# A query tile's fetch later in SyncE's queue, and one output projection a pair group later, in a fused attention and feed-forward block

## The chip, the core and the metric

The kernel runs on one core of one Trainium2 chip. The metric is the device time of one execution in microseconds (us); a lower one is better. The engines are named as in the profile: PE (TensorE) multiplies matrices into PSUM, DVE (VectorE), ACT (ScalarE) and POOL (GpSimd) do elementwise work, and SP (SyncE) issues most of the transfers (DMA), in the order in which they stand in its queue. Matrices in SBUF and PSUM lie on 128 partitions. PSUM has 8 banks; `pair(i)` in the code is banks 2i and 2i+1.

## The reference

One transformer block over S = 2048 rows of D = 576 values, all in bf16. Cut to what matters:

```python
mod = silu(c) @ w_mod            # six rows of 576: sa, ca, ga, sb, cb, gb
h = layernorm(x) * (1 + ca) + sa
q, k, v = split(h @ wqkv)        # 32 heads of 18
phi(u) = concat(softmax(u @ w_phi), softmax(-(u @ w_phi)))   # 36 features per head
kv = phi(k)^T v ;  z = sum(phi(k))
o = (phi(q) @ kv) / (phi(q) @ z + 1e-6)
x = x + ga * (o @ wo)
h = layernorm(x) * (1 + cb) + sb
x = x + gb * (relu(h @ w1) @ w2)        # 576 -> 4608 -> 576
```

The attention is linear: all keys and values are first summed into one small matrix `kv` per head, and then each row of queries needs only that matrix. So a tile of rows can go through its attention and its feed-forward part without the other tiles, once `kv` is complete.

## The kernel before, in words

The 2048 rows are 16 tiles of 128, taken two by two in 8 blocks (b = 0 to 7). The program has two parts.

The first part is a list of small jobs in a hand-written order (`ORDER`, L44). It loads everything, makes the features of the keys and of all queries, sums `kv`, and takes tiles 0 and 1 through attention, output projection and second layer norm. The features of the queries (`eq(u)` for query tile u) do not all fit in SBUF. From tile 4 on they go out to DRAM (`q_out`, L334) and come back by `q_in(u)` (L337, in the profile `RT<-eqd`, L338) into one of three buffers, number u % 3. So query tiles 4 and 7 share a buffer. `q_fin(u)` (L351) does what turns a fetched tile into an operand: `q_sm` sums the features on DVE (L283, L342), `q_pool` multiplies on POOL (L345, L290), and `q_turn` has a DMA transpose issued by SP (L349, `RE<-RT`; 9 chunks of 128 columns).

The second part is a loop over the blocks. `l1` (L694) is the first feed-forward layer: nine groups u = 0 to 8, each of 36 matmuls (L682) into one PSUM pair, followed by `relu`, which reads that pair with ACT (L690, L691) and DVE (L692). `l2` (L720) is the second layer, written as seven half-size products (L729) with sums of weight parts as operands; DVE makes those sums (`t_part`, L465, and L707, L737). The attention of a later block's two tiles is threaded into this by hooks: a hook is called ahead of each group of `l1` and at each ninth matmul of `l2`, and what it emits stands at that place in every engine's order.

For a tile t the steps are: `attend(t)`, that is `num_mm` on PE (L390) and `num_o` on DVE (L397, L398), which leave the attention's result in o_sb; `o_turn(t)`, a small copy on ACT (L794) and a DMA transpose issued by SP (L402, `oT<-o_sb`; 5 chunks); `project`, the output projection on PE (`wo_full`, L800, 16 matmuls for two tiles, and `wo_rest`, L807, 4 matmuls); `add_res`, the residual sum on DVE (L412); `bn` (L239, L240) and `norm2`, the second layer norm, which ends with another DMA transpose (L402, `h<-xn`).

In block 0 the hook is `b0_l1` (L833). Before group u = 0 and u = 1 it calls `q_next(4)` and `q_next(5)` (L780). `q_next` first issues the fetch that the call before left in `held`, then does `q_fin`, then notes the next fetch. So `q_next(4)` does `q_fin(4)` and notes 7; `q_next(5)` does `q_in(7)`, then `q_fin(5)`, and notes 8. SP's order there is: transpose of query tile 4 (`q_turn(4)`), `q_in(7)`, `q_turn(5)`, and then at u = 3 `o_turn(2)` and `o_turn(3)`. `q_in(7)` writes the buffer that `q_turn(4)` reads. At u = 6 the hook projects tiles 2 and 3 into pairs 2 and 0, ahead of the group's matmuls, and at u = 7 it adds the residuals. The nine groups of block 0 use the pairs 2, 0, 2, 0, 1, 3, 1, 3, 2 (L890). In the later blocks the hooks `in_l1` and `in_l2` do the same steps at other places, with `project` between the blocks (L893).

No scheduler moves anything: each engine takes its instructions in the order in which the program text emits them, and waits on semaphores where data is not yet there.

Of the kernel before, what the change touches and what calls it, by code (L numbers as in the profile page):

```python
# [62 lines left out]
def tile_block(ctx, tc, a, out):  # L63
# [22 lines left out]
    NEQ, NE, NV, NL = 6, 5, 4, 3  # L86
# [70 lines left out]
    def pair(i):  # L157
        return PS[:, 2 * i:2 * i + 2, :]
# [77 lines left out]
    def bn(n, t):  # L236
        s = st[:, t % 4]
        for hf in range(2):
            dve.bn_stats(out=s[:, hf, :], in_=x_sb[:, t, hf * HD:(hf + 1) * HD])  # L239
        dve.bn_aggr(out=mv[:, n, t, :], in_=s)  # L240
# [96 lines left out]
    def q_in(u):  # L337
        sp.dma_start(EL[:, u % NL, :], eqd[:, u, :])  # L338

    def q_sm(u):  # L340
        sums(eq(u), Rq[:, u % 2, :])
        dve.reciprocal(out=rq[:, u % 2, :], in_=hs(Rq[:, u % 2, :], 1))  # L342

    def q_pool(u):
        pool.tensor_tensor(out=ratq[:, u % 2, :], in0=hs(Rq[:, u % 2, :], 0), in1=rq[:, u % 2, :], op=ALU.mult)  # L345
        minus(pool, eq(u), ratq[:, u % 2, :])

    def q_turn(u):
        sp.dma_start_transpose(ET[:, u % NET], eq(u).rearrange("p (c f) -> p c f", f=P))  # L349

    def q_fin(u):  # L351
        q_sm(u)
        q_pool(u)
        q_turn(u)
# [55 lines left out]
    def add_res(t, pr):  # L410
        x = v2(x_sb[:, t, :])
        dve.tensor_tensor(out=x, in0=x, in1=pr[:, :, 0:HD], op=ALU.add)  # L412
# [48 lines left out]
    def t_part(i, k):  # L461

        j = slice(6 * k, 6 * k + 6)
        eng, o, p, q = ((dve, T1, B12, B11), (dve, T2, B22, T1), (dve, T4, B21, T2), (dve, T3, B12, B22))[i]
        eng.tensor_tensor(out=o[:, j, :], in0=p[:, j, :], in1=q[:, j, :], op=ALU.subtract)  # L465
# [312 lines left out]
    held = []  # L778

    def q_next(q):  # L780

        if held and held[0] < NT:
            q_in(held[0])
        del held[:]
        if q < NT:
            q_fin(q)
            held.append(q + NL)

    def attend(t, pr):
        num_mm(t, pr)  # L790
        num_o(t, pr)

    def o_turn(t):
        act.activation(out=o_sb[:, t % 2, D:640], in_=o_sb[:, t % 2, 512:D], func=ACT.Copy)  # L794
        turn_dma(oT[:, t % 2], o_sb[:, t % 2, :])
# [14 lines left out]
    def project(t, prs):  # L810
        for i in range(2):
            wo_full(t + i, prs[i])
        for i in range(2):
            wo_rest(t + i, prs[i])
# [5 lines left out]
    def norm2(t):  # L820
        ln2_rs(t)
        ln2_apply(t)
        i = t % 2
        turn_dma(h2[:, t // 2 % 2, :, i * P:(i + 1) * P], xn[:, i, :])
# [7 lines left out]

    def b0_l1(u):  # L833
        if u < 2:
            q_next(4 + u)
        if u == 2:
            attend(2, pair(1))
            attend(3, pair(3))
        if u == 3:
            o_turn(2)  # L840
            o_turn(3)
        if u in (0, 3, 4):
            t_part(1, (0, 3, 4).index(u))
        if u in (5, 6):
            t_part(3, u - 5)
        if u == 6:
            project(2, (pair(2), pair(0)))
        if u == 7:
            add_res(2, pair(2))
            add_res(3, pair(0))  # L850
            bn(1, 2)
        if u == 8:
            bn(1, 3)
            norm2(2)
# [34 lines left out]
    for b in range(NB):  # L889
        l1(b, (2, 0, 2, 0, 1, 3, 1, 3, 2) if b == 0 else (2, 1, 0, 3, 2, 1, 0, 3, 2), in_l1(b) if b else b0_l1)  # L890
        l2(b, in_l2(b))
        if b + 2 < NB:
            project(2 * b + 4, WO)  # L893
# [103 lines left out]
```

## Time and profile before

| | us |
|---|---|
| median of 3 timed runs | 391.26 |
| lowest and highest | 390.72, 391.53 |
| the profiled execution | 390.21 |
| its span, first to last instruction | 388.4 |
| PE busy in it | 379.6 |
| DVE busy in it | 238.1 |

The profile is of one execution. Times in its rows are us from the start of the span; a row of the timeline gives start, duration, engine, line, operation, the tiles written and read, and how often. A bracket at its end gives how long the engine had been idle and who released it. Block 0's first layer lies at about 92 to 118 us, its second layer at about 118 to 134; the later blocks follow one after another, some 36 us each. In rows of windows the columns are the stretch, its length, the busy time of PE, PEld (the loading of weights), DVE, ACT and POOL with the number of instructions, then the granted clock of PE as a share of full speed, the mean busy share of the 16 DMA engines and the GB/s that they moved.

### The profile page before, as it was taken

The page shows a single profiled execution, that of the slowest core. Times are in us where ns is not written, and L with a number is a line of the kernel's source. Part 1 is how long each engine was busy: PE and PEld are TensorE (multiplying, and loading weights), DVE is VectorE, ACT ScalarE, POOL GpSimd, SP SyncE. Part 2 cuts the span into 40 slices and gives each one's busy share as a digit, 9 for nine tenths or more (in the row PEclk, how much of TensorE's full clock was granted, in tenths as well). Part 3 has the DMA queues.
Part 4 walks back from the last instruction along what each step waited for, and adds up shares of the span by engine and source line. Part 5 has one row for each costly group of instructions (what it writes and reads, how often), then busy time and mean ns, then how long its engine had stood idle before and what let it go on. Part 6 is the DMA issues. An engine that isn't in the chain of part 4 may idle for free.

```text
span 388.4 us, 11401 instructions
## 1 busy us (share of the span) xinstructions
PE 379.6 (98%) x4901; PEld 313.3 (81%) x4901; DVE 238.1 (61%) x439; ACT 186.5 (48%) x449; POOL 123.7 (32%) x195
## 2 busy tenths in 40 slices
PE   8999999999799999999999999999999999999996
PEld 4877788888668788788888887887788888878875
DVE  2899998788929568527743872596177526422243
ACT  2789997689413544505631571256045505622410
POOL 2078889831101402230232124123303230042023
PEclk9999999999989999999999999999999999999999
DMA  7995799798903108401710342064207103001000
GB/s 301 420 417 200 264 385 358 138 251 272 154 19 71 42 17 128 91 32 37 152 34 32 93 95 34 32 108 95 35 19 115 44 30 47 19 0 35 2 2 30
DMA packets 56276, 45.16 MB, mean 116 GB/s; under 512 B 46625, under 2 KB 49314, under 8 KB 55458
## 3 DMA queue, kind: packets, MB, share of 16 engines
q1 hardware_dynamic: 55938, 44.25, 42.2%
q8 instruction: 38, 0.62, 0.7%
q10 hardware_dynamic: 288, 0.19, 0.2%
q14 instruction: 12, 0.10, 0.1%
HBM read 27.38 MB, written 5.90 MB: 86 GB/s over the span
## 4 chain that ended last, share of the span: by engine, by line
PE 86%; DMA 5%; ACT 3%; DVE 3%; issue 1%; POOL 1%; SPq 0%; POOLq 0%; DVEq 0%
PE PS L682 36%; PE PS L729 31%; PE PS L273 10%; PE PS L800 4%; DMA x_sb<-in_xk_dram 2%; ACT RT L278 2%; PE PS L390 2%; DMA R<-in_wkT_dram 2%; DMA oT<-o_sb 1%; PE PS L323 1%; DVE Rk L283 1%; PE PS L807 1%; PE PS L407 1%; DVE st L239 1%; ACT RT L511 0%
## 5 line engine op out<-in xcount | busy, mean ns | idle before, releaser
L682 PE MATMUL PS<-h,R 64*128 64x256 bf16 (+1 forms) x2628 | 143.7, 268 | 0.0
L682 PEld LDWEIGHTS <-R 64*128 64x128 bf16 x2628 | 126.6, 94 | 16.0 <-issue 0.5
L729 PEld LDWEIGHTS <-RH 128*128 128x128 f16 x846 | 81.7, 98 | 21.9 <-issue 1.7
L690 ACT ACTIVATE RH<-PS 128x256 f16<-128x256 f32 x72 | 27.8, 386 | 130.4 <-PE PS L682 130.3
L729 PE MATMUL PS<-R,RH 128*128 128x288 bf16 (+1 forms) x558 | 73.2, 286 | 0.0
L717 POOL TENSOR_TENSOR yt<-yt,gb_row 128x288 f32<-128x288 f32 x23 | 24.9, 1082 | 142.5 <-DVE yt L716 142.5
L692 DVE SCALAR_TENSOR_TENSOR RH<-PS,RH 128x256 f16<-128x256 f32 x72 | 29.6, 415 | 47.4 <-ACT RH L690 47.4
L278 ACT ACTIVATE RT<-PS,rs 128x576 bf16<-128x576 f32 x64 | 42.9, 747 | 2.2 <-PE PS L273 1.8
L691 ACT ACTIVATE RH<-PS 128x512 f16<-128x512 f32 x72 | 42.7, 594 | 0.0
L716 DVE TENSOR_TENSOR yt<-PS,RS 128x288 f32<-128x288 f32 x23 | 10.5, 456 | 46.5 <-PE PS L729 46.5
L729 PE MATMUL PS<-RT,RH 128*128 128x288 f16 x288 | 37.9, 286 | 0.0
L829 ACT ACTIVATE h<-h,mod 128x256 bf16<-128x256 bf16 x63 | 32.8, 590 | 0.0
L273 PE MATMUL PS<-RH,R 116*128 116x288 bf16 x240 | 32.5, 286 | 0.2 <-DVE RH L519 0.2
L345 POOL TENSOR_TENSOR ratq<-Rq,rq 128x32 f32<-128x32 f32 x16 | 4.8, 298 | 87.3 <-DVE rq L342 87.3
L273 PE MATMUL PS<-RH,RT 116*128 116x288 bf16 x240 | 31.9, 286 | 0.2 <-ACT RT L278 0.2
L239 DVE BATCH_NORM_STATS2 st<-x_sb 128x6 f32<-128x288 bf16 x64 | 25.8, 444 | 3.4 <-DMA x_sb<-in_xk_dram 3.4
L273 PEld LDWEIGHTS <-R 116*128 116x128 bf16 x240 | 22.7, 98 | 6.2 <-issue 0.6
L273 PEld LDWEIGHTS <-RT 116*128 116x128 bf16 x240 | 22.9, 98 | 5.8 <-issue 0.3
L733 ACT ACTIVATE RS<-PS 128x288 f32<-128x288 f32 x24 | 9.9, 411 | 32.6 <-PE PS L729 32.6
L718 POOL TENSOR_TENSOR x_sb<-yt,x_sb 128x288 bf16<-128x288 f32 x31 | 22.7, 731 | 5.8 <-DVE yt L714 4.0
L283 DVE TENSOR_REDUCE Rq<-RT 128x64 f32<-128x1152 bf16 x16 | 21.5, 1344 | 0.9 <-DMA RT<-eqd 0.9
L283 DVE TENSOR_REDUCE Rk<-RT 128x64 f32<-128x1152 bf16 x16 | 21.3, 1336 | 0.9 <-ACT RT L278 0.7
(117 smaller groups left out, 414.1 us busy)
## 6 DMA issues: line engine op xcount, KB each, us to landing
R<-in_w_dram SPq DMA_DIRECT2D x4, 1152.0 KB, 8.4
eqd<-RT SPq DMA_DIRECT2D x12, 288.0 KB, 2.1
RT<-eqd SPq DMA_DIRECT2D x12, 288.0 KB, 3.1
R<-in_w2b_dram SPq DMA_DIRECT2D x2, 1296.0 KB, 8.1
R<-in_w2a_dram SPq DMA_DIRECT2D x3, 864.0 KB
out_dram<-x_sb SPq DMA_DIRECT2D x15, 144.0 KB, 1.7
RT<-in_xT_dram SPq DMA_DIRECT2D x2, 640.0 KB
x_sb<-in_xk_dram SPq DMA_DIRECT2D x3, 288.0 KB, 7.7
```

Of the source, the lines that this page charges most:

```text
L239: dve.bn_stats(out=s[:, hf, :], in_=x_sb[:, t, hf * HD:(hf + 1) * HD])
L273: pe.matmul(pr[:, k, 0:HD], lhsT=xt(t, ck), rhs=w[0:R, ck, k * HD:(k + 1) * HD], start=(ck == 0), stop=(ck == NC - 1))
L278: act.activation(out=E.rearrange("p (b h s e) -> p b h s e", b=2, s=2, e=DH)[:, :, :, s, :], in_=pr[:, :, 0:HD].rearrange("p b (h e) -> p ...
L283: dve.tensor_reduce(out=Rr, in_=E.rearrange("p (c e) -> p c e", e=DH), axis=AXX, op=ALU.add)
L682: pe.matmul(PS[:, 2 * u + hf, n * 256 + o:n * 256 + o + w], lhsT=w1[b0:b0 + 64, c, j * P:(j + 1) * P], rhs=hb[b0:b0 + 64, c, o:o + w], sta ...
L690: act.activation(out=A11[:, j, :], in_=lo[:, :, 0, :], func=ACT.Relu)
L691: act.activation(out=A2[:, j, :, :], in_=PS[:, 2 * u + 1, :].rearrange("p (n s f) -> p n s f", n=2, s=2), func=ACT.Relu)
L692: dve.scalar_tensor_tensor(out=U3[:, j, :], in0=lo[:, :, 1, :], scalar=0.0, in1=A11[:, j, :], op0=ALU.max, op1=ALU.subtract)
L717: pool.tensor_tensor(out=y, in0=y, in1=gb_row[:, c], op=ALU.mult)
L718: pool.tensor_tensor(out=x_sb[:, t, c], in0=y, in1=x_sb[:, t, c], op=ALU.add)
L729: pe.matmul(PS[:, bank, 0:HD], lhsT=am[:, j, :], rhs=bm[:, j, :], start=first and j == 0, stop=(j % 9 == 8), skip_group_check=True)
L829: act.activation(out=o, in_=o, func=ACT.Identity, scale=mod(1, c), bias=mod(0, c))
```

## The change

```diff
     def b0_l1(u):
         if u < 2:
-            q_next(4 + u)
+            q_fin(4 + u)
+        if u == 5:
+            q_in(7)
+            held.append(5 + NL)
         if u == 2:
             attend(2, pair(1))
             attend(3, pair(3))
...
         if u in (5, 6):
             t_part(3, u - 5)
-        if u == 6:
+        if u == 7:
             project(2, (pair(2), pair(0)))
-        if u == 7:
             add_res(2, pair(2))
             add_res(3, pair(0))
             bn(1, 2)
```

At u = 0 and u = 1 the hook now does only `q_fin(4)` and `q_fin(5)`. The fetch `q_in(7)` comes at u = 5, and `held` holds 8 from there on as before, so the later blocks see no difference. SP's order becomes `q_turn(4)`, `q_turn(5)`, `o_turn(2)`, `o_turn(3)`, `q_in(7)`. On PE the 20 matmuls of the projection of tiles 2 and 3 move from before the 36 matmuls of group u = 6 to behind them. The order of instructions on DVE, ACT and POOL is the same as before, and no instruction is added or left out. Some semaphores that name a transfer change their number, since they are dealt out in SP's order.

## The prediction

> **What bounds the kernel now.** I read the page first, for the busy shares and the 40 slices.
>
> ```profile
> PE 379.6 (98%) x4901; PEld 313.3 (81%) x4901; DVE 238.1 (61%) x439; ACT 186.5 (48%) x449; POOL 123.7 (32%) x195
> ...
> PE   8999999999799999999999999999999999999996
> ...
> PEclk9999999999989999999999999999999999999999
> ```
>
> TensorE (PE) is busy 98% of the span, and only slice 11 of its row (97.1 to 106.8 us) shows a real hole; the granted clock, PEclk, is below 9 in one slice alone, the next. Time can be gained only in that hole, or by shortening PE's own work. The view of PE's waits over the whole span names the hole: one wait of 2.9 us, for the DMA transpose that fills oT. The next waits are 1.3 us (the kernel's start) and 0.3.
>
> ```profile
> PE PS L800 <- DMA oT<-o_sb: 2.9, 1, 2.9
> PE PS L234 <- POOL eps_t L226: 1.3, 1, 1.3
> PE PS L258 <- ACT RT L278: 0.3, 1, 0.3
> ```
>
> PE's timeline there (start, duration) shows that the first-layer groups u=2 to 5 end at 96.74 + 8.03 = 104.77. Then PE waits until 107.71, when `project(2)` begins.
>
> ```profile
> 96.74 8.03 PE L682 MATMUL PS<-h,R 64*128 64x256 bf16 x144
> 107.71 3.03 PE L800 MATMUL PS<-wo_sb,oT 128*128 128x288 bf16 x16 [2.94 <-DMA oT<-o_sb]
> ```
>
> The chain that ended last gives the stretch without overlaps. The first four rows are this block, the last three the same pieces one block on: 16 + 4 projection matmuls and 9 groups (324 matmuls).
>
> ```profile
> 107.71 3.03 PE PS L800 x16
> 110.74 0.59 PE PS L807 x4
> 111.33 6.38 PE PS L682 x108
> 117.72 2.31 PE PS L729 x18
> ...
> 134.01 1.96 PE PS L800 x16
> 135.97 0.35 PE PS L807 x4
> 136.32 17.68 PE PS L682 x324
> ```
>
> So the same work is slower after the hole. The projection takes 3.03 + 0.59 = 3.62 instead of 1.96 + 0.35 = 2.31, and three groups take 6.38 instead of 17.68 / 3 = 5.89 (one group: 1.96). The windows give the reason in PEclk, the granted clock (the figure behind the POOL column):
>
> ```profile
> 104.77:107.71 2.94, 0.00 (x1) 0.00 (x0) 2.25 (x4) 0.87 (x2) 0.00 (x0) 1.00 1.21 125
> 107.71:111.33 3.62, 3.62 (x22) 2.22 (x24) 0.00 (x0) 0.00 (x0) 0.00 (x0) 0.65 0.00 0
> 111.33:117.72 6.39, 6.39 (x110) 5.33 (x106) 3.45 (x9) 2.24 (x6) 0.00 (x0) 0.93 0.01 3
> 134.00:136.32 2.32, 2.32 (x25) 1.70 (x24) 0.54 (x2) 0.00 (x0) 1.46 (x2) 1.00 0.18 64
> ```
>
> After the hole the clock is 0.65 for 3.62 us and 0.93 for 6.39: 3.62 x 0.35 + 6.39 x 0.07 = 1.7 us lost, against 1.80 by the durations. One block on, without a hole, it is 1.00.
>
> **Why the transpose is late.** SyncE (SP) issues in order. Its timeline (start, time of issuing):
>
> ```profile
> 97.54 1.32 SPq L349 DMA_TRANSPOSE RE<-RT  x1
> 101.42 0.33 SPq L338 DMA_DIRECT2D RT<-eqd  x1
> 101.85 1.28 SPq L349 DMA_TRANSPOSE RE<-RT  x1
> 103.23 3.21 SPq L402 DMA_TRANSPOSE oT<-o_sb  x2
> ```
>
> These are `q_turn(4)`, `q_in(7)`, `q_turn(5)` and the two `o_turn`. SP's own waits say what held the second: it waited 2.5 us until the transpose of `q_turn(4)` had landed (`q_in(7)` overwrites the buffer that this reads). All behind it had been ready earlier: GpSimd (POOL) ended the product for `q_turn(5)` at 98.55 + 1.17 = 99.72, and ScalarE (ACT) the two o_sb rows at 99.93 and 100.82.
>
> ```profile
> SPq L338 <- DMA RE<-RT: 2.5, 1, 2.5
> ```
> ```profile
> 98.55 1.17 POOL L290 TENSOR_TENSOR RT<-RT,ratq 128x576 bf16<-128x576 bf16 x1
> ```
> ```profile
> 99.67 0.26 ACT L794 ACTIVATE o_sb<-o_sb 128x64 bf16<-128x64 bf16 x1
> 100.56 0.26 ACT L794 ACTIVATE o_sb<-o_sb 128x64 bf16<-128x64 bf16 x1 [0.63 <-DVE o_sb L398]
> ```
> ```profile
> 103.23 4.44 DMA oT<-o_sb
> ```
>
> The last row, from the chain, is tile 2's transpose: 4.44 us from issue to 107.67.
>
> **The change part by part.** No instruction is added or removed; VectorE (DVE), ACT and POOL keep their order. Two things move.
>
> *`q_in(7)` behind both `o_turn`.* It is moved past three DMA transposes in SP's queue; nothing moves past POOL's. SP is free of `q_turn(4)` at 97.54 + 1.32 = 98.86, so `q_turn(5)` goes when POOL is done: 99.75 to 101.03. The `o_turn` of tile 2 follows 0.10 later (the gap between 101.85 + 1.28 and 103.23), at 101.1: 2.1 us earlier. Half of the 3.21 us that issuing both took puts tile 3's at 102.7. Landing is bounded from two sides. This tile over the whole run, in the view of its instructions, landed 2.4 us after its issue in the middle and 3.7 at most where it was counted; the row above has 4.44.
>
> ```profile
> DMA to landing us min/median/max: 2.4/2.4/3.7
> ```
>
> That gives 103.5 to 105.6 for tile 2 and 105.1 to 107.1 for tile 3. I keep the late ends, since the transposes still run behind one another. `q_in(7)` is then issued at about 104.3, its own wait (landing at 101.4) long over. Its 288 KB are late for nobody: DVE's sum of query tile 7 runs at 150.58 in block 1, and SP has nothing behind it until the h transposes at 119.16. If its packets slowed tile 3's transpose, the slack worked out below covers 0.6 us; beyond that it is paid in full.
>
> ```profile
> 150.58 1.34 DVE L283 TENSOR_REDUCE Rq<-RT 128x64 f32<-128x1152 bf16 x1
> ...
> 119.16 4.21 SPq L402 DMA_TRANSPOSE h<-xn  x2
> ```
>
> *`project(2)` from u=6 to u=7.* PE goes straight from 104.77 into group u=6, until 104.77 + 1.96 = 106.73. That group writes PSUM pair 1, whose last reader is DVE's part of group u=4, ended at 103.69 + 0.42 = 104.11: 0.66 us in hand. The projection then needs tile 2 at 106.73 (1.1 us after the late end) and tile 3 half of 1.96 later, at 107.71 (0.6 after). So I cost its wait at nothing. The cover is u=6's 1.96 us; without it tile 3's late end alone would stall PE by over a microsecond.
>
> What comes late next? The projection ends at 106.73 + 2.31 = 109.04. DVE's two `add_res` now run right behind it, and the first must have read pair 2 before u=8 writes that pair at 109.04 + 1.96 = 111.00. DVE is ready: its `t_part` of this hook ends at 107.36, and its part of u=6 (ACT ends 0.38 after 106.73, then 0.42) at 107.8.
>
> ```profile
> 103.69 0.42 DVE L692 SCALAR_TENSOR_TENSOR RH<-PS,RH 128x256 f16<-128x256 f32 x1
> ...
> 106.31 1.05 DVE L465 TENSOR_TENSOR R<-R,R 128x1728 f16<-128x1728 bf16 x1
> 114.24 0.42 DVE L692 SCALAR_TENSOR_TENSOR RH<-PS,RH 128x256 f16<-128x256 f32 x1 [6.88 <-ACT RH L690]
> 114.58 1.41 DVE L412 TENSOR_TENSOR x_sb<-x_sb,PS 128x576 bf16<-128x576 bf16 x2
> ...
> 121.97 1.35 DVE L737 TENSOR_TENSOR RH<-RT,RH 128x2304 f16<-128x2304 f16 x1
> ```
>
> Half of 1.41 after 109.05 is 109.8: 1.2 us in hand. Further on, DVE runs dense from 114.58 to 123.32, when L737 has made the operand for the product that PE starts at 125.02: 1.70 us in hand. After, the same 8.74 us run from 109.05 to 117.8, and PE asks at 125.02 - 4.75 = 120.27: 2.5 us in hand, so I cost it at nothing.
>
> ```profile
> 125.02 1.14 PE L729 MATMUL PS<-RT,RH 128*128 128x288 f16 x8
> ```
>
> **The sum.** From 104.77 to the second layer's start, before: 117.72 - 104.77 = 12.95. After: three groups 5.89, projection 1.96 + 0.35 = 8.20. Gain 4.75 us: 2.94 of waiting and 1.8 of slow clock. Behind it PE waits for nothing to the end, so the gain stays. The profiled execution took 390.21 us (span 388.4 and 1.81 around it) and would take 385.5. The three timed runs have the median 391.26 (390.72 to 391.53), 1.05 above it; the stretch is the same work in each, so I take 4.75 from the median: **386.5 us**.
>
> **A rule that speaks against part of it.** The row with 0.65 follows 2.94 us of idleness. The Trainium skill, page "TensorE: Matmul & The Clock Gate", section "What's actually happening", says that the clock halves after at least one idle window of about 3.4 us. By that reading 2.94 us would not be enough, the drop would have another cause and stay, and the sum would be 2.94 instead of 4.75. The trace has the drop right behind its one hole and nowhere else (the PEclk row above), which speaks for the hole as its cause.
>
> **The rivals.**
>
> *The transposes, and not SP's queue, set the landing.* The DMA share in the windows is 0.66 for 98 to 103 and 1.10 for 103 to 108, so the engines were not idle while SP waited.
>
> ```profile
> 98.00:103.00 5.00, 5.00 (x97) 4.46 (x94) 4.84 (x11) 2.30 (x7) 1.42 (x2) 1.00 0.66 95
> 103.00:108.00 5.00, 2.06 (x37) 1.58 (x32) 4.02 (x6) 1.58 (x4) 0.00 (x0) 1.00 1.10 170
> ```
>
> If tile 2 lands at 107.67 as now, the first half of the change does nothing for the time. PE then waits 107.71 - 106.73 = 0.98 us: 387.5. Against it: the 0.66 leaves 1.7 us of five unused, and 288 KB leave the way.
>
> *The clock falls all the same.* Its rows are 1.00 in the hole itself and 0.65 only once PE runs again, so another cause than the hole is not shut out. Then only 2.94 is gained: 388.3. The rule above would lead here.
>
> *Slower: four transposes back to back hinder each other.* With the plain fetch gone from between them, the two 9-chunk and the two 5-chunk transposes run without a break, and the wait returns at u=7 with only two groups left behind it. With the slow clock (1.80) the second layer then starts at s + 2.31 + 3.92 + 1.80 for a projection start s, and meets today's 117.72 at s = 109.69. It is slower by over 0.2% (0.8 us, about what a measurement of this kernel can tell from no change) from s = 110.5. At a landing of 111.0 it costs 1.3 us: 392.6. Tile 2 would have to take 9.4 us from its issue at 101.1, over twice the longest row. The same mechanism with s near 109.7 gives no change, 391.3.
>
> **How the numbers follow.** Forecast 386.5: 0.77. Landing unchanged, 387.5: 0.09. Slow clock stays, 388.3: 0.05. No change: 0.03. Slower, 392.6: 0.06. The forecast's own range is 385.6 to 387.2 (the runs' spread of -0.5 and +0.3 about their median, and some 0.4 for the sum). To hold the two partial cases it reaches up to 388.4: **385.6 to 388.4**. Faster by over 0.2%: 0.77 + 0.09 + 0.05 = 0.91; within: 0.03; slower: 0.06.
>
> **What would show it.** Right: slice 11 of the PE row full, no wait of L800 for oT, granted clock 1.00 from 104 to 118, `project(2)` near 106.7 in 2.3 us, the second layer near 113.0, SP's two `o_turn` near 101.1 and 102.7 with `q_in(7)` behind them. Wrong: a wait of L800 at u=7 (then see whether SP's issue or the landing is late), of L682 at u=8 for DVE, of L729 for L737, or a clock below 1.00 without a hole ahead of it.

## The result and the profile after

The changed kernel takes 386.01 us (median of 4 runs, 385.82 to 386.73) against 390.99 for the kernel before in the same comparison (4 runs, 390.66 to 391.53): 4.98 us less, a ratio of 0.9875 with a 95% interval of 0.9856 to 0.9893. The predicted time was 386.5. A second comparison gave 385.84 against 390.88, a ratio of 0.9867 (0.9838 to 0.9897). Ratios here and below are worked out from the single runs and need not be quotients of the medians; they leave out a run in the slow state, of which there was one (398.22 us, the kernel before, beside e5 and e6). The profiled execution took 385.86 us with a span of 384.1.

The page of the kernel after has no hole in its PE row any more, and the granted clock stays at full tenths:

```profile
PE   8999999999999999999999999999999999999995
...
PEclk9999999999999999999999999999999999999999
```

PE's waits over the whole span no longer name oT. What is left is the kernel's start and two waits of 0.2 us in its first part:

```profile
PE PS L234 <- POOL eps_t L226: 1.3, 1, 1.3
PE PS L258 <- ACT RT L278: 0.2, 1, 0.2
PE PS L273 <- ACT RT L278: 0.2, 1, 0.2
```

SP's timeline of the kernel after shows the new order, `q_turn(4)` and `q_turn(5)`, both `o_turn`, then `q_in(7)`:

```profile
96.62 4.14 SPq L349 DMA_TRANSPOSE RE<-RT  x2
100.87 2.57 SPq L402 DMA_TRANSPOSE oT<-o_sb  x2
103.54 0.53 SPq L338 DMA_DIRECT2D RT<-eqd  x1
```

And the chain of the kernel after runs on PE alone, from the groups u=2 to 6 (180 matmuls) into the projection, two more groups, and the second layer:

```profile
96.89 9.93 PE PS L682 x180
106.83 2.07 PE PS L800 x16
108.89 0.35 PE PS L807 x4
109.24 3.93 PE PS L682 x72
113.17 2.31 PE PS L729 x18
```

The second layer starts at 113.17 instead of 117.72: 4.55 us earlier of the 4.75 forecast. The projection's first part took 2.07 us instead of 1.96, and the stretch began 0.08 later (96.89 against 96.81 in the chain before). The windows of the kernel after give the clock for this stretch (the figure ahead of the DMA share):

```profile
104.00:118.00 14.00, 14.00 (x193) 11.42 (x190) 11.66 (x22) 4.67 (x13) 0.00 (x0) 1.00 0.21 50
```

### The profile page after: what moved, and what is told of

It is laid out like the page before. It is cut to its first block, busy times and chain, and to the rows that moved or that the text cites. A ratio compares the mean times of both kernels' runs of the same rounds, so it can differ in the third digit from the quotient of the medians.

```text
span 384.1 us, 11397 instructions
## 1 busy us (share of the span) xinstructions
PE 378.2 (98%) x4899; PEld 313.1 (82%) x4901; DVE 239.2 (62%) x439; ACT 186.2 (48%) x449; POOL 123.2 (32%) x195
## 4 chain that ended last, share of the span: by engine, by line
PE 90%; ACT 4%; DMA 2%; DVE 2%; issue 1%; POOL 1%; SPq 0%; POOLq 0%; DVEq 0%; ACTq 0%
PE PS L682 37%; PE PS L729 31%; PE PS L273 11%; PE PS L800 4%; ACT RT L278 2%; DMA R<-in_wsh_dram 2%; PE PS L390 2%; PE PS L323 1%; PE PS L250 1%; PE PS L807 1%; PE PS L407 1%; PE PS L258 0%; ACT RT L511 0%; DVE RT L304 0%; DVE st L239 0%
```

## The experiments

The theory: SP's queue made the transposes of tiles 2 and 3 late, PE idled for them, and the idleness halved its clock for a while. The change removes the lateness, and the later projection covers what is left of it. The rivals: the transposes themselves set the landing; the bytes of the fetch cost, not its wait; the clock falls for another reason. Each time is a median; ratios are to the kernel before on the same chip.

| kernel | us (range) | ratio (95%) | PE's wait for oT in its profile |
|---|---|---|---|
| e1, only the fetch moved | 386.65 (385.96 to 387.04) | 0.9888 (0.9868 to 0.9908) | none |
| e2, only the projection moved | 387.46 (386.83 to 387.79) | 0.9912 (0.9890 to 0.9933) | 1.2 |
| e3, hole filled with zeros | 389.01 (388.94 to 389.10) | 0.9953 (0.9935 to 0.9972) | 0.2 |
| e4, fetch into a buffer of its own | 388.22 (386.95 to 390.00) | 0.9944 (0.9917 to 0.9971) | 0.6 and 0.8 |
| e5, fetch ahead of both `o_turn` | 387.36 (386.63 to 388.11) | 0.9895 (0.9861 to 0.9929) | 1.1 |
| e6, hole half filled | 389.41 (388.62 to 391.38) | 0.9946 (0.9920 to 0.9972) | 1.5 |
| e7, before, PE's stream shifted | 389.60 (388.08 to 390.88) | 0.9974 (0.9952 to 0.9995) | 2.2 |
| e8, after, PE's stream shifted | 386.06 (385.81 to 387.15) | 0.9891 (0.9863 to 0.9919) | none |
| e9, e1 with PE's stream shifted | 387.50 (386.74 to 388.56) | 0.9917 (0.9887 to 0.9947) | 1.0 |

Beside them the kernel before had medians of 390.77 (e1 to e4), 392.32 (e5 and e6; here it spread from 389.40 to 398.22), 390.89 (e7 and e8) and 390.88 (e9).

### Each half of the change alone (e1, e2)

```diff
# e1
         if u < 2:
-            q_next(4 + u)
+            q_fin(4 + u)
+        if u == 5:
+            q_in(7)
+            held.append(5 + NL)
# e2
-        if u == 6:
+        if u == 7:
             project(2, (pair(2), pair(0)))
-        if u == 7:
             add_res(2, pair(2))
```

> Only the fetch of query tile 7 moves behind both o_turn; project(2) stays at u=6. My theory (SP's queue made the transposes late): in the changed kernel tile 2 was ready by the semaphore at about 104.3 and tile 3 at 104.9, and PE asks for them at 104.85 and 105.85 here, so PE does not wait and the clock stays at 1.00: 386.0 us, at most 386.8 if a late landing leaves up to 0.8 us of waiting. Rival (the move of the projection carries the gain, the landing is set by the transposes): tile 2 still lands near 107.7, the hole and the slow clock stay, 391.0 us.

> Only project(2) moves to u=7; the fetch of tile 7 stays ahead of query tile 5's transpose in SP's queue. My theory: tile 2 lands at 107.67 as before, PE asks at 106.75, a hole of 0.9 to 1.0 us; if so short a hole leaves the clock at 1.00, 387.0 us; if it halves the clock for the window after it, 1.7 us more, 388.7 us. Rival (the projection's place does not matter): 391.0 us. Rival (landings come earlier when PE is busy): 386.0 us.

Both went as the theory said. The chain of e1 goes from the group u=5 straight into the projection; nothing waits:

```profile
96.56 7.97 PE PS L682 x144
104.53 2.07 PE PS L800 x16
106.60 0.35 PE PS L807 x4
106.95 5.89 PE PS L682 x108
```

The chain of e2 still has the transpose, with the same 4.43 us from issue to landing as before, but PE meets it a group later:

```profile
103.19 4.43 DMA oT<-o_sb
107.62 0.05 issue
107.66 2.13 PE PS L800 x16
109.80 0.35 PE PS L807 x4
```

A hole of 1.2 us is left (0.9 to 1.0 was expected) and the clock stays at 1.00 (the projection takes 2.13 + 0.35). So moving the fetch alone brings 4.1 us of the 5.0, moving the projection alone 3.3, and together they don't add up: they are two ways to remove the same hole.

### What the clock is worth (e3, e6, and the kernel before twice more)

```diff
# e3; e6 has 6 in place of 13
         if u == 6:
+            spin(13, 4)
             project(2, (pair(2), pair(0)))
```

`spin` multiplies zeros into a bank that the projection overwrites.

> The kernel before with 13 matmuls of zeros (512 columns, 0.21 us each, 2.8 us in all) put ahead of project(2), into a bank that the projection overwrites: the wait for oT stays, but PE is busy in most of it. Theory (the hole causes the slow clock): granted clock 1.00 throughout, projection in 2.31 and three groups in 5.89 us, gain 1.8: 389.2 us. Rival (the clock falls for another reason): 391.0 us.

> The kernel before with 6 matmuls of zeros ahead of project(2) (1.3 us), so that a hole of about 1.6 us is left. Theory (the clock follows how idle a stretch of some 3.4 us was, and 2.9 us is not the least that does it): if 1.6 us is enough, the clock falls as before and the time is 391.0; if not, it stays at 1.00 and the time is 389.2. Both outcomes bound the least hole: between 1.6 and 2.9 us for the second, below 1.6 for the first.

> The kernel before, once more. Theory (the clock is set by how idle a fixed stretch of 3.4 us was, and these stretches lie by chance against the hole): the hole is 2.9 us again; the clock after it falls in some executions (391 us) and may stay at 1.00 in others (389.2). Rival (a hole of 2.9 us always halves it): 391 us and a clock of 0.996.

> The kernel before, a third profile. As for the second: the hole of 2.9 us in each; either 391 us with the slow clock or 389.2 us without it.

With the hole filled, the projection still starts late, but at full clock. The chain of e3:

```profile
108.15 2.13 PE PS L800 x16
110.28 0.35 PE PS L807 x4
110.64 5.89 PE PS L682 x108
```

The time falls by 390.77 - 389.01 = 1.76 us (1.1 to 2.5 by the interval of the ratio). That is the clock's share on the average, 1.8 in the forecast, and it shows that the hole causes the drop. In one execution the share is not 1.8, though. The kernel before, profiled twice more (b1 and b2), took 389.41 and 392.63 us. The expectation of a hole of 2.9 us in each failed. In b1 the hole is 2.5 us and the windows show no drop:

```profile
104.80:107.30 2.50, 0.00 (x0) 0.00 (x0) 1.86 (x3) 0.87 (x2) 0.00 (x0) 1.00 0.89 99
107.30:115.70 8.40, 8.38 (x129) 6.92 (x130) 3.53 (x10) 2.24 (x6) 0.00 (x0) 1.00 0.01 2
```

In b2 the hole is 3.5 us, and the clock is 0.72 over the 10.70 us behind it; the projection alone takes 4.02 us in its chain.

```profile
104.80:108.30 3.50, 0.03 (x1) 0.03 (x2) 2.15 (x4) 0.87 (x2) 0.00 (x0) 0.87 1.12 126
108.30:119.00 10.70, 10.70 (x123) 7.80 (x124) 2.96 (x8) 1.98 (x5) 0.00 (x0) 0.72 0.00 0
```

The clock records of the trace give half speed for 3.41 us in the execution of the prediction, for none in b1 and for 6.83 us in b2: 0, 1 or 2 pieces of 3.41 us. One piece costs half of its length, 1.7 us. The two of b2 cost some 2.8, since they began while PE still idled: in its chain the projection and three groups take 11.21 us, in that of b1 8.37.

The same records say why the cost is a matter of chance. The changes of the clock lie on a grid of 3.41 us (in the execution of the prediction 101.96, 105.37, 108.79). PE was idle for 2.3 us of the grid's stretch ahead of the drop there and for 2.6 us of that in b2. In the profiles with a hole and no drop it was idle for at most 1.5 us of any one stretch of block 0; the hole of 2.5 us in b1 is cut into 1.0 and 1.5. The end of a run, behind PE's last instruction, has such drops too and adds cases. Over all fourteen profiles the clock fell behind each of the 16 stretches at full speed in which PE was idle for 1.99 us or more, and behind none of those with 1.97 or less. So what decides is where the hole falls on the grid, and not its length alone. Back to full speed it went behind a stretch without idleness (twice); behind one with 0.9 us, in b2, it stayed at half, which is the second piece.

The holes of 2.2 us (e7) and 1.5 us (e6) had no drop in their profiles. Their timed runs did not all escape it. A piece of 3.41 us at half speed lowers the mean clock of such a run by 0.004, and the mean was 0.994 or 0.995 in 8 of e7's 12 runs and 0.996 in 2 of e6's 12, the two slowest (390.53 and 391.38), against 0.998 to 1.000 in the rest. How long the hole was in these runs is not on record; by the limit of 2 us a hole of 1.5 would not be enough.

### The wait or the bytes of the fetch (e4)

```diff
+    def el(u):
+        return NL if u == 7 else u % NL
     def q_in(u):
-        sp.dma_start(EL[:, u % NL, :], eqd[:, u, :])
+        sp.dma_start(EL[:, el(u), :], eqd[:, u, :])
```

`eq` reads the same buffer, and the memory behind `EL` is one buffer longer. Nothing is moved.

> The kernel before, in its order, but query tile 7 is fetched into a fourth buffer, so that its fetch no longer waits for the transpose of query tile 4. Nothing is moved. Theory (it is the wait in SP's queue that costs, not the 288 KB): query tile 5's transpose is issued near 99.8 and tile 2's near 101.1; the 288 KB ahead of them take some 0.7 us of the DMA engines, tile 2 lands at 104.9 to 105.6, PE asks at 104.8: a hole of 0.1 to 0.8 us, clock 1.00, 386.1 to 386.9 us. Rival (the bytes ahead of the transposes cost as much as the wait): tile 2 lands at 106.5 or later, a hole of 1.7 us or more and part of the slow clock, 388 to 391 us.

SP's timeline of e4 shows the wait gone: the fetch at 98.64, `q_turn(5)` at 99.32, the first `o_turn` at 101.36.

```profile
98.64 0.57 SPq L341 DMA_DIRECT2D RT<-eqd  x1
99.32 1.94 SPq L352 DMA_TRANSPOSE RE<-RT  x1
101.36 2.56 SPq L405 DMA_TRANSPOSE oT<-o_sb  x2
```

But PE waits twice, for tile 2 and then for tile 3, as its timeline in e4 says:

```profile
105.27 1.16 PE L803 MATMUL PS<-wo_sb,oT 128*128 128x288 bf16 x8 [0.61 <-DMA oT<-o_sb]
107.25 1.15 PE L803 MATMUL PS<-wo_sb,oT 128*128 128x288 bf16 x8 [0.82 <-DMA oT<-o_sb]
```

Tile 2 landed at 105.23, as the theory said, and PE waited 0.6 us for it. The time of 388.22 misses the theory's 386.1 to 386.9 and falls to the lower end of the rival's 388 to 391. Taking the wait away brings 2.6 us with the fetch still ahead of the transposes; it does not bring all. In the profiles tile 2 lands 2.4 us earlier than before without the wait (107.67 and 105.23), and 1.2 us earlier still with the fetch behind the transposes (104.05 in e1). Tile 3's landing, nearly 6 us after the first of the two was issued, was nothing that the theory had a reason for. A landing has 16 records in the trace: 15 of tile 3's came by 105.67, the last at 107.20. A fetch of 16 KB of instructions had started at 105.05. This led to the next runs.

### What else delays a transpose (e5, e7, e8, e9)

e5 is the changed kernel with the fetch at u=2 instead of u=5, that is ahead of both `o_turn`.

```diff
-        if u == 5:
+        if u == 2:
             q_in(7)
             held.append(5 + NL)
```

> The changed kernel, but the fetch of tile 7 stands between query tile 5's transpose and the two o_turn. It still waits until query tile 4's transpose has landed (101.4 to 101.6), so tile 2's transpose is issued near 102.0 instead of 101.1 and lands 2.4 to 4.4 us later, at 104.4 to 106.4; PE asks at 106.8. Theory (the projection's new place is slack of 2 us that covers this): no wait, 386.0 us. Rival (the fetch must stand behind both o_turn): PE waits at u=7, 386.5 to 388.

This expectation failed: there is a wait of 1.1 us at u=7, and tile 2's transpose took 5.47 us in the chain of e5, against 4.44 in the kernel before.

```profile
102.26 5.47 DMA oT<-o_sb
107.73 0.05 issue
107.78 2.13 PE PS L800 x16
```

The DMA view of that stretch shows what happened. Its 40 slices run from 103 to 109 us, 0.15 us each: the transposes stop at about 106.0, move 5 to 10 GB/s at most until 107.3, and end then. In the same view one fetch of instructions runs, 16 KB on queue 8; the packet records place it at 105.3.

```profile
GB/s 31 46 61 169 246 384 355 285 311 294 249 171 56 15 108 361 270 270 154 19 7 0 0 0 5 9 10 9 10 99 91 0 0 0 0 0 0 0 0 0
...
q8 instruction: 1, 0.02, 1.4%
```

The kernel before has the same pattern where its hole lies. In its view of the same 6 us the transposes stand nearly still from about 105.4 to 106.7, behind a fetch that the packet records place at 104.86; tile 2's landing at 107.67 lies behind this.

```profile
GB/s 138 276 384 362 341 266 268 183 186 292 283 299 364 266 278 104 36 0 0 2 7 10 10 9 10 202 284 288 292 219 0 0 0 0 0 0 0 0 0 0
...
q8 instruction: 1, 0.02, 1.2%
```

It has it elsewhere too. First the view of 195 to 201 us, two `oT` transposes without such a fetch (its only queue line is q1), then 231 to 237, where one falls into the first of two:

```profile
GB/s 0 0 0 0 0 0 0 0 0 0 0 24 227 292 290 232 28 0 0 0 0 0 0 0 0 0 0 0 0 0 0 0 164 287 288 280 74 0 0 0
...
q1 hardware_dynamic: 1344, 0.33, 24.3%
```

```profile
GB/s 0 0 0 0 0 0 0 0 0 0 109 0 0 32 225 275 261 68 7 10 9 10 9 160 26 0 0 0 0 0 0 0 0 5 188 288 288 266 57 0
...
q8 instruction: 1, 0.02, 1.1%
```

The first is one burst of 0.7 us; the second stands nearly still for 0.75 us in its middle. Counted from the packet records of all fourteen profiles, behind 117 us: of 142 such transposes without a fetch on queue 8 in the microsecond ahead of them or during them, 136 took 0.72 to 0.77 us from the first to the last packet; of 26 with one, 25 took 1.2 to 3.2.

A smaller fetch does it as well. Near 102 us every profile has one of 8 KB on queue 14. In the six in which transposes were then under way (the kernel after twice, e1, e4, e8, e9) they stand nearly still for 0.75 to 0.9 us just behind it. The view of 101 to 105 us of the kernel after, in slices of 0.1 us, shows this from 102.7 to 103.5; the packet records place the fetch at 102.41.

```profile
GB/s 292 289 292 282 253 287 266 248 215 218 162 192 259 266 323 271 110 26 8 10 8 8 8 8 8 77 255 289 292 297 287 223 198 0 0 164 46 161 115 46
...
q14 instruction: 1, 0.01, 0.5%
```

To move the fetches on purpose, the 12 warm-up matmuls of zeros at the start became 48 of a quarter of the width:

```diff
-        "Z": lambda i: spin(i, 6),
+        "Z": lambda i: spin(4 * i, 6, 128),
```

> The kernel before, with the 12 warm-up matmuls of zeros at its start replaced by 48 of a quarter of the width: the same warm-up time, but 72 more PE instructions, so that every 16 KB piece of PE's instruction stream is fetched 72 instructions (about 2 us) earlier relative to the work. In the kernel before such a fetch runs at 98.4 and at 104.9, each while DMA transposes are under way, and these then stand still for about a second microsecond. Theory (the instruction fetches hold up the transposes and are part of the late landing): query tile 4's transpose is no longer caught and lands about 2.8 us after its issue instead of 3.8, all behind it follows about 1 us earlier, PE's hole at project(2) shrinks from 2.9 to 0.5 to 1.8 us and the clock stays at 1.00: 387.0 to 388.5 us. Rival (the fetches have nothing to do with it): the hole stays at 2.9 and the time at 391.

> The changed kernel with the same replacement. The fetch that ran at 104.5, just behind the last transpose, now runs near 102.6, in the middle of the transposes of tiles 2 and 3. Theory: they are held up by 1 to 1.4 us and land at 104.9 to 106.2; PE asks at 106.8 and 107.8, so the 2 us of the group u=6 cover it: no wait, 386.0 us. Rival (the change lives from the place of the fetch): PE waits at u=7, 387 us or more.

> Only the fetch of tile 7 is moved (project(2) stays at u=6), with the warm-up of 72 more PE instructions. With these the changed kernel's transposes were held up and tile 2 landed at 106.2, tile 3 at 107.0, where without them it was 104.3 and 104.9. PE asks at 104.8 and 105.8 here. Theory (the projection's later place is cover against late landings and nothing else): a wait of 1.2 to 1.7 us, clock at 1.00, 387.2 to 387.9 us, against 386.0 with the projection at u=7. Rival (the projection's place is worth nothing in any case): 386.0 to 386.5 us.

> The changed kernel once more, on the chip of the run beside it: no wait of the projection, clock at 1.00, 386.0 us.

By the packet records the fetches at 98.4 and 104.9 of the kernel before ran at 96.5 and 103.9 in e7: PE's instruction stream is what they bring. `q_turn(4)` was no longer caught and had no standstill; it landed 3.4 us after its issue, before 3.8. The 2.8 that was expected is less than any of the 140 such transposes behind 117 us took in the fourteen profiles (3.2 at least). And its issue was 0.3 us later. The second fetch, moved by 1.0 us and not by 2, still fell among the transposes, which stood still from 104.1 to 105.6 (105.3 to 106.8 in the kernel before). PE's wait shrank to 2.2 us, not to 0.5 to 1.8, and the time to 389.60 instead of 387.0 to 388.5: the right direction, too large a size. Part of the miss is the clock, which was forecast at 1.00: the four runs without a drop took 388.08 to 388.55 us, the eight with one 389.16 to 390.88.

e8 and e9 are the cleaner pair. In both, the transposes of tiles 2 and 3 are held up, in e8 from 104.0 to 105.4 (the fetch ran at 103.5, where 102.6 was expected). In e8 the landing records end at 105.70 and 106.33 us (104.31 and 104.97 in the kernel after); the 106.2 and 107.0 in the expectation of e9 are later than these records, and so its wait of 1.2 to 1.7 us was set too high. With the projection at u=7, PE asks at 106.74 and does not wait:

```profile
103.90 2.84 PE PS L682 x52
106.74 2.07 PE PS L800 x16
```

With the projection at u=6, in e9, PE's timeline has the wait:

```profile
106.06 2.13 PE L800 MATMUL PS<-wo_sb,oT 128*128 128x288 bf16 x16 [1.00 <-DMA oT<-o_sb]
```

386.06 and 387.50 us against 390.89 and 390.88. When a fetch on queue 8 falls into the transposes, the second half of the change saves the wait of 1.0 us that e9's profile has; the medians lie 1.4 apart, with ranges that overlap a little. In the place that the fetch has without the shift the second half is worth less: e1's 386.65 lies 0.6 above the changed kernel's 386.01, and the ranges overlap. The place is near the edge, though. In the profile of the changed kernel beside e9 (385.84) the fetch started at 104.54, and the last of tile 3's 16 landing records came at 106.68. With the projection at u=6 PE would have asked for tile 3 near 105.6; as it is, it asked near 107.6.

## Why the prediction was right, point by point

- **What bounds the kernel.** Right: PE, and one hole of 2.9 us in the execution that was read (2.5 and 3.5 in b1 and b2). The chain of the kernel after has only PE from the group u=2 into the second layer.
- **SP's order.** Right. The two `o_turn` went at 100.87 and about 1.3 later (forecast 101.1 and 102.7), `q_in(7)` at 103.54 (104.3).
- **The landing.** Good enough for the sum, wrong as a bound, and helped by luck. Tile 2 landed at 104.31, inside 103.5 to 105.6, and tile 3 at 104.97, just ahead of 105.1 to 107.1. Tile 2 landed 3.36 us earlier than before: 2.36 by the earlier issue, which is the wait in SP's queue, and 1.00 because it took 3.44 us and not 4.44. But 4.44 us was no upper end: e5's transpose took 5.47. What stretched the transposes was a fetch of instructions, which the prediction did not see. In the kernel before, the 16 KB at 104.86 held up the transposes for some 1.5 us. In the kernel after, the 8 KB at 102.41 did so for 0.9, and the transposes of both tiles had moved their data just ahead of the 16 KB at 104.52. That place is luck; the slack at u=7 is not. With the fetch among them (e8) tile 2 still landed 1.0 us before PE asked, close to the 1.1 of the forecast.
- **The wait moved to u=7 costs nothing.** Right; no wait of L800, also in e8. Of the two moves, the cover of the group u=6 is the one that holds when the landing is late, up to its 2 us: in e5, with tile 2 landing at 107.73, 1.1 us of waiting came through.
- **DVE behind the projection.** Right: `add_res` ran at 109.16 (109.05), and L737 ended at 118.16 for a product at 120.48, 2.3 us in hand (2.5). From the timelines of the kernel after, DVE and then PE:

```profile
109.16 1.42 DVE L412 TENSOR_TENSOR x_sb<-x_sb,PS 128x576 bf16<-128x576 bf16 x2 [1.38 <-PE PS L807]
...
116.81 1.35 DVE L737 TENSOR_TENSOR RH<-RT,RH 128x2304 f16<-128x2304 f16 x1
```

```profile
120.48 1.27 PE L729 MATMUL PS<-RT,RH 128*128 128x288 f16 x9
```

- **The sum.** 4.75 forecast, 4.55 in the two profiles up to the second layer, 4.35 in the profiled executions (385.86, where 385.5 was forecast), 4.98 in the medians. The 1.8 of slow clock is right as a mean (e3: 1.76); in one execution it is 0, 1.7 or some 2.8. So the 1.05 us between the profile and the median of the kernel before, which the prediction carried over because the stretch is the same work in each run, did not carry over: the changed kernel has no hole to vary, and its profile and its median are 0.15 apart. That this and the smaller gain of the profile partly cancel is luck. The kernel before ran anywhere from 388.3 to 392.9 us beside e1 to e4 and e7 to e9, while the changed one stayed within 385.6 to 386.7.
- **The rule on the clock.** The Trainium skill, page "TensorE: Matmul & The Clock Gate", section "What's actually happening", asks for an idle window of about 3.4 us and says that the windows run freely. Its window length agrees with the slow pieces of 3.41 and 6.83 us. That they run freely agrees with the grid of 3.41 us, against which the hole lay differently in each profile. Its least idleness does not agree: a hole of 2.9 us was enough, in the execution of the prediction, with PE idle for 2.3 of the 3.41 us ahead of the drop, and e3 shows the hole to be the cause. In the fourteen profiles 2 us of idleness in one stretch were enough.
- **The rivals.** The first, 387.5 if the landing stayed at 107.67, was run as e2 and gave 387.46, so its price was right and its condition wrong. The slow clock without a hole: no run had it. Transposes hindering each other until PE waits at u=7: not in the kernel after; e5 shows the place and a small size, 1.1 us, with a fetch of instructions among the transposes.

The later blocks took 0.2 us more in the profile after than before (from the second layer of block 0 to PE's end); that was not followed up.

## What to carry to other kernels

Before a transfer that may have to wait is put into an in-order queue, ask what stands behind it and when that is due: here 2.5 us of waiting for a buffer that nobody needed for over 45 us held up the transposes on which PE depended. A consumer that can be moved one group later buys cover against every cause of lateness up to the length of that group (here 2 us), also causes not known; reordering the queue removes only the one that is known. An idle hole in PE may cost more than its length, and by chance: its price is a mean over executions, so look at more than one profile.

## What the runs showed of the hardware

A fetch of PE's instructions (16 KB, queue 8) held up the DMA transposes under way: a 5-chunk transpose took 1.2 to 3.2 us from first to last packet in 25 of 26 cases with one, 0.72 to 0.77 in 136 of 142 without. One of 8 KB on queue 14 held them up for 0.75 to 0.9 us in six profiles of six. Why they do was not tried. The clock after an idle hole was halved in pieces of 3.41 us: in the profiles none after 1.0 to 2.5 us of idleness, one after 2.9, two after 3.5. Each length was seen in single profiles only. Counted by stretches of the 3.41 us grid, with the runs' ends, the clock fell behind all 16 with 1.99 us of idleness or more and behind none with 1.97 or less.
